# Two heads of batch 0's keys by the hardware queues in place of four, w_in ahead of batch 1's keys, and a new order of the work

## The chip, the cores and the metric

The kernel runs on one core of one Trainium2 chip. Five engines work side by side: PE (matmuls; it also spends time on loading weights), DVE and ACT (elementwise work; both can read PE's results), POOL (GpSimd) and SP. Transfers from and to the chip's memory are issued by SP and ACT (the hardware queues) and by POOL (GpSimd's queue, which can convert float32 to bfloat16 on the way). The metric is the device time of one execution in microseconds; the time before is the median of three runs.

## The reference

Eight batches of eight heads with 576 rows of 64 go through two attentions and a feed-forward layer. In the first attention 32 learned rows p ask the keys and values; its result serves as keys and as values for the second attention, in which the queries ask. The heads are then put side by side, which gives 4608 rows of 512, and pass through w_in, an activation, and w_out.

```
p_packed = sm_attn(p, k, v)            # softmax(scale * p k^T) v, 32 rows per head
out      = sm_attn(q, p_packed, p_packed)
x = out.transpose(0, 2, 1, 3).reshape(B * S, H * D)
h = x @ w_in
g = where(h >= 1, h, where(h <= -1, 0, (h + 1)**2 / 4))
return g @ w_out
```

All inputs and the output are float32; the kernel computes with bfloat16 operands.

## The kernel before

All of q, k, v, w_in and w_out is converted to bfloat16. For each batch b the steps, by the names of the tiles, are:

- `kT`, `qT`: keys and queries with the head dimension on the partitions. For batches 0 and 1 PE transposes them into a PSUM tile `tp` (in the functions `turned`, L377), and DVE and ACT copy the halves out. From batch 2 on SP issues a transposing transfer.
- `sp`, `ex`, `pk`, `ppT`: scores of p against the keys (L431), their exponentials on ACT (L437), and the pack, i.e. the product with the values, and the row sums (L476 to L486), copied out as `ppT`.
- `s`, `eT`, `sm`, `ln`, `rc`, `A`: scores of the queries against the packed rows (L516), exponentials (ACT, L556), their sums by a matmul with ones (L561), a reciprocal by logarithm and exponential (ACT, L565, L570), and the normalized weights `A` (DVE, L575), for the two groups g of heads.
- `mp`, `M`: the packed rows times w_in (L529), in four quarters f of 512 columns, copied out as `M` (helper `copy`, L197). The product of attention and w_in is thus taken as `A` times `M`, and the attention's output itself is never formed.
- `h`, `x`, `t`, `hT`: for each of 16 slices fi of 128 of the 2048 columns, four matmuls of `M` and `A` (L649), two steps of the activation on ACT or ACT and DVE (x, L655; t, L663 on DVE or L665 on ACT), and a last one on DVE (hT, L670). Slices 0 to 3 need quarter 0 of M, 4 to 7 quarter 1, and so on.
- `o`, `ob`: 36 output tiles of 128 rows, each 16 matmuls of hT with w_out (L723), copied out and stored by SP (L741). Slices 0 to 3 need quarter 0 of w_out, and so on.

The PSUM is divided into three wide tiles (`w`), which `tp`, `sp`, `pk`, `s`, `sm`, `mp`, `h` and a few output tiles (those in `LENT`) take in turns, and two narrow ones (`o`). A wide tile is free again when the copy or the activation that reads it has ended.

The order of the work on each engine is not written out. Every step is a `Task` with a rank, the engines that could do it with a cost on each, and the steps that it needs; `Plan.run` plays through them with these costs and fixes one list per engine, which each engine then works off in order. The ranks come from the constants `H1`, `H2`, `T1`, `T2`, `EARLY` and so on. Where PE has nothing to do in the plan before the first output matmul, the function `warm` puts in matmuls of zeros (L791), as many as fill the planned gap.

The loads stand in the order of `LOADS`, one list on POOL's queue. In before it is k0 (its heads 4 to 7), v0, q0 (three pieces), k1, w_in quarters 0 (two halves), v1, and so on. Heads 0 to 3 of batch 0's keys, and p for batches 0 and 1, are loaded ahead of them as float32 by the hardware queues, two heads by SP and two by ACT (`k_raw`, L317), and converted by DVE and ACT (`casts`). There is one buffer for keys (`k`), so that k1's load waits until k0's transposes are done. `MB0` and `MB1` are costs of single loads in the plan; they change what the plan expects, not the transfer.

Of the kernel before, what the change touches and what calls it, by code (L numbers as in the profile page):

```python
# [121 lines left out]
def kernel(  # L122
# [11 lines left out]
    f32 = mybir.dt.float32  # L134
# [4 lines left out]
    B, H, S, D = q.shape  # L139
# [8 lines left out]
    G, Q, TP, X = 2, 4, 96, 2  # L148
    NC = S // TP
# [3 lines left out]
    FW = 512  # L153
    NF = d_ff // FW
    SPAN = 28.0
    MB0 = {("k", 0, 4): 1.07, ("v", 0, 0): 1.35, ("q", 0, 0): 0.5}
    MB1 = {("w_in", 0, 0): 0.7, ("w_in", 0, 1): 0.7}
    FIRST = 2
    PAIRED = 2
    SPLIT, AHALF, WPARTS, MPARTS, QLATE, ORDER3, ORDER, MERGE = 0, 0, 1, 3, 0, 0, 2, 3  # L160
    Q0 = [range(0, 8, 2), range(1, 5, 2), range(5, 9, 2)]
    LOADS = "k0 v0 q0 k1 win0 v1 win1 win2 wout0 wout1 win3 wout2 q1 wout3 v2 q2 p k2"
    H1, H2 = 26.53, 38.72
    PITCH0, PITCH1 = 0.56, 0.33
    T1, T2 = -11.47, 25.95
    LENT = [1, 8]
    L1, M1 = -14.28, 5.97
    KT1, QT1 = -33.50, -6.64
    SC1, PK1 = 25.09, -6.06
    ST1, MT1 = 12.93, 25.80  # L170
    EARLY = [[(27.88, 73.23), (29.26, 41.94), (45.63, 29.37), (44.78, 16.76)], [(54.77, 7.14), (14.06, 35.17), (62.97, 47.75), (30.5, 10.14), (23.52, 36.85)]]

    V, A_, G_ = nc.vector, nc.scalar, nc.gpsimd
    nc.scalar.preload_act_table_set("natural_log_exp_and_others")
# [1 line left out]
    BUFS = dict(w=3, o=2, k=1, q=2, v=1, vv=1, kT=2, qT=2, ex=2, ppT=2, M=2, A=2, eT=4, ln=2, rc=2, x=4, t=4, ob=4)  # L176
    const = ctx.enter_context(tc.tile_pool(name="const", bufs=1))
    work = ctx.enter_context(tc.tile_pool(name="work", bufs=1))
# [7 lines left out]
    def new(tag, shape, dtype):  # L186
        return work.tile(shape, dtype, tag=tag, name=tag, bufs=BUFS[tag])

    plan = Plan(dict(BUFS, dma=8))
# [14 lines left out]
    def either(dve, act, *pairs, parted=None):  # L204

        def emit(e):
            for to, of in pairs:
                copy(e, to(), of(), parted)
        return {"DVE": (dve[0], dve[1], emit), "ACT": (act[0], act[1], emit)}
# [1 line left out]

    p_raw = work.tile([NP, 2, H, D], f32, tag="k1", name="p_raw", bufs=1)
    p_nat = const.tile([NP, B, H, D], bf16)
    k_raw = work.tile([TP, 4, NC * D], f32, tag="q", name="k_raw", bufs=BUFS["q"])
    w_in_sb = const.tile([P, Q, d_ff], bf16)
    w_out_sb = const.tile([P, KF, d_model], bf16)
    w_in_v = moe_w_in.rearrange("(a p) f -> p a f", p=P)
# [22 lines left out]
    landed = {}  # L240
# [9 lines left out]
    def dma(key, rank, emit, mb, takes=(), settle=0.9):  # L250
        t = plan.add(rank, {"DMA": (0.78, 2.1, emit, mb / 0.405, settle)}, takes=list(takes) + ["dma"])
        plan.release("dma", [t])
        chain("loads", t)
        landed[key] = t
        if key == ("v", 0, 0):
            chain("loads", identity)
        return t

    def tokens(nm, b):
        if (nm, b) not in have:  # L260
            have[nm, b] = new(nm, [TP, H, NC, D], bf16)
        return have[nm, b].rearrange("p h c d -> p h (c d)")

    def heads(hs):
        return slice(hs[0], hs[-1] + 1, hs.step)

    def rows_of(nm, b, hs):
        return {"k": k, "q": q, "v": v}[nm][b, heads(hs)].rearrange("h (p c) d -> p h (c d)", c=NC)

    def load(nm, b, rank):  # L270

        for i, hs in enumerate({("k", 0): [range(4, 8)], ("q", 0): Q0}.get((nm, b), [range(H)])):
            def emit(e, hs=hs):
                G_.dma_start(tokens(nm, b)[:, heads(hs)], rows_of(nm, b, hs))  # L274
            mb = MB0.get((nm, b, hs[0]), (1.18 if b < 2 else 1.3) * len(hs) / H)
            t = dma((nm, b, hs[0]), rank + 0.01 * i, emit, mb, [nm] if i == 0 else [], 0.9 if b < 2 else 1.7)
            for h in hs:
                landed[nm, b, h] = [t]
# [16 lines left out]

    for n, what in enumerate(LOADS.split()):
        if what[:-1] == "win":
            load_w_in(int(what[-1]), -1000 + n)
        elif what[:-1] == "wout":
            load_w_out(int(what[-1]), -1000 + n)  # L300
        elif what == "p":
            load_p(-1000 + n)
        else:
            load(what[0], int(what[1]), -1000 + n)
    for b in range(3, B):
        for n, nm in enumerate(["kqv", "kvq", "qkv", "qvk", "vkq", "vqk"][ORDER3 if b == 3 else ORDER]):
            load(nm, b, -960 + 10 * b + n)
# [5 lines left out]
    p_first = plan.add(-1000, {"SP": (1.0, 3.3, load_p_raw)})  # L313

    def load_k_raw(e):
        for i, queue in enumerate((nc.sync, nc.scalar)):
            queue.dma_start(k_raw[:, 2 * i:2 * i + 2], rows_of("k", 0, range(2 * i, 2 * i + 2)))  # L317

    k_first = plan.add(-999, {"SP": (1.0, 4.3, load_k_raw)}, behind=[p_first])
    casts = [plan.add(-30.2 + 0.1 * i, either(  # L320
        (0.5, 0.55), (0.8, 0.85), (lambda i=i: tokens("k", 0)[:, 2 * i:2 * i + 2], lambda i=i: k_raw[:, 2 * i:2 * i + 2])),
        [k_first], behind=landed["k", 0, 4]) for i in range(2)]
    for h in range(4):
        landed["k", 0, h] = casts


    pT_of = {}
# [379 lines left out]
    def output(pr, i, rank, pitch, parts=1):  # L707


        w = d_model // parts  # L710
        lent = pr == 0 and i in LENT
        bs = sorted({2 * pr + i * P // S, 2 * pr + ((i + 1) * P - 1) // S})
# [46 lines left out]
    def evenly(n, start, span):  # L759
        return [(start + span / n * j, span / n) for j in range(n)]  # L760

    for b in range(B):
# [8 lines left out]
        first = 0 if b % 2 == 0 else 4  # L771
        for j, (start, span) in enumerate(EARLY[b] if b < len(EARLY) else evenly(4 + b % 2, base[b] + SPAN, SPAN)):
            parts = 2 if (b, first + j) == (B - 1, 8) else 1
# [53 lines left out]
```

## Time and profile before

| | us |
|---|---|
| median of three runs | 246.61 (246.17 to 246.77) |
| the profiled execution, its own time | 248.54 |
| its span, first to last instruction | 246.8 |
| PE busy | 239.2, 97% |
| ACT busy | 199.0, 81% |
| DVE busy | 177.0, 72% |
| first h matmul | 23.32 |
| first o matmul | 32.51 |
| last matmul's end | 243.0 |
| mean granted clock of PE | 0.993 |

The engines' busy times and the chain of waits are those of one profiled execution. A matmul's end is modelled, so that matmuls of one group overlap in the rows; the distance from one start to the next is what PE spends on it. Rows of windows give busy times in a stretch of the span; rows of the timeline give start, duration, engine, line, operation, output tile and input tiles, count, and in brackets the idle time ahead and what ended it.

### The profile page before, as it was taken

What the parts mean: (1) busy time and instruction counts of PE and PEld (TensorE: products, weight loads), DVE (VectorE), ACT (ScalarE), POOL (GpSimd) and SP (SyncE); (2) the same over time, 40 slices, a digit from 0 to 9 for tenths busy, and PEclk for the clock granted to TensorE, in tenths of its full rate; (3) what the DMA queues carried; (4) which work ended last, traced back from release to release, by engine and by line L of the source; (5) the groups of instructions that cost most, each with busy time, mean ns of one, the idle gap of its engine ahead of it and who ended that gap; (6) DMA issues with size and microseconds to landing.
All of it is one profiled execution on the core that took longest, in us unless ns stands there. A gap on an engine that the chain in (4) does not pass through costs nothing.

```text
span 246.8 us, 5485 instructions
## 1 busy us (share of the span) xinstructions
PE 239.2 (97%) x2221; PEld 137.6 (56%) x2221; DVE 177.0 (72%) x299; ACT 199.0 (81%) x329; POOL 29.0 (12%) x42
## 2 busy tenths in 40 slices
PE   8979999999999999999999999999999999999993
PEld 2745555465654665566556646655665455555453
DVE  4425996588966997799889859957995877776000
ACT  3575997899989989999899799979988998886111
POOL 7463410000500120021021001100000000000000
PEclk9997999999999999999999999999999999999999
DMA  7999999969999999999999959976721111122223
GB/s 162 201 204 206 206 206 205 194 119 155 161 215 240 199 168 224 174 141 218 234 139 215 177 104 147 181 129 120 137 63 46 43 45 43 44 51 77 54 76 85
DMA packets 59195, 35.85 MB, mean 145 GB/s; under 512 B 31905, under 2 KB 54689, under 8 KB 59169
## 3 DMA queue, kind: packets, MB, share of 16 engines
q0 software_dynamic: 24256, 18.25, 49.9%
q1 hardware_dynamic: 34208, 16.69, 32.1%
q10 hardware_dynamic: 704, 0.56, 0.8%
q8 instruction: 17, 0.28, 0.5%
q14 instruction: 10, 0.07, 0.1%
HBM read 37.22 MB, written 9.44 MB: 189 GB/s over the span
## 4 chain that ended last, share of the span: by engine, by line
PE 87%; DMA 6%; ACT 4%; DVE 1%; issue 0%
PE o L723 49%; PE h L649 25%; DMA k<-in_k_dram 4%; PE mp L529 3%; PE sp L431 2%; DMA k_raw<-in_k_dram 2%; PE pk L476 2%; PE tp L377 1%; PE o L791 1%; PE sm L561 1%; PE s L516 1%; DVE M L197 1%; ACT x L655 1%; PE pk L486 1%; ACT eT L556 1%; ACT rc L570 1%
## 5 line engine op out<-in xcount | busy, mean ns | idle before, releaser
L723 PE MATMUL o<-w_out_sb,hT 128*128 128x512 bf16 (+1 forms) x592 | 146.9, 373 | 0.0
L670 DVE SCALAR_TENSOR_TENSOR hT<-t 128x576 bf16<-128x576 f32 x128 | 93.8, 753 | 9.1 <-ACT t L665 7.0
L655 ACT ACTIVATE x<-h 128x576 f32<-128x576 f32 x128 | 79.1, 659 | 10.9 <-PE h L649 9.5
L723 PEld LDWEIGHTS <-hT 128*128 128x128 bf16 x592 | 55.6, 98 | 48.2 <-issue 4.9
L649 PE MATMUL h<-A,M 128*128 128x288 bf16 x512 | 79.0, 286 | 0.4 <-DVE M L197 0.4
L649 PEld LDWEIGHTS <-M 128*128 128x128 bf16 x512 | 49.5, 98 | 29.2 <-issue 1.4
L665 ACT ACTIVATE t<-x 128x576 f32<-128x576 f32 x63 | 43.8, 695 | 1.1
L663 DVE TENSOR_SCALAR t<-x 128x576 f32<-128x576 f32 x65 | 30.8, 473 | 9.7 <-ACT x L655 9.5
L197 ACT CAST M<-mp 128x1024 bf16<-128x1024 f32 (+1 forms) x24 | 22.7, 977 | 3.5 <-PE mp L529 3.4
L197 DVE COPY ob<-o 128x512 f32<-128x512 f32 x24 | 16.4, 688 | 7.8 <-PE o L723 7.6
L575 DVE SCALAR_TENSOR_TENSOR A<-eT,rs,rc 128x576 bf16<-128x576 bf16 x16 | 12.9, 816 | 9.0 <-ACT rc L570 9.0
L197 ACT COPY ob<-o 128x512 f32<-128x512 f32 (+1 forms) x13 | 7.2, 557 | 14.6 <-PE o L723 14.3
L274 POOL DMA_DIRECT2D k<-in_k_dram x8 | 6.5, 811 | 104.7 <-DMA kT<-k 81.1
L791 PE MATMUL o<-zeros 128*128 128x512 bf16 (+1 forms) x45 | 13.8, 421 | 1.2 <-DVE zeros L227 1.2
L437 ACT ACTIVATE ex<-sp 96x768 bf16<-96x768 f32 x16 | 12.5, 804 | 2.6 <-PE sp L431 2.6
L197 DVE CAST M<-mp 128x1024 bf16<-128x1024 f32 (+1 forms) x11 | 11.2, 1025 | 1.3 <-PE mp L529 1.3
L556 ACT ACTIVATE eT<-s,rs 128x576 bf16<-128x576 f32 x16 | 11.0, 744 | 0.7 <-PE s L516 0.7
L529 PE MATMUL mp<-w_in_sb,ppT 64*32 64x512 bf16 x256 | 11.3, 387 | 0.0
L570 ACT ACTIVATE rc<-ln 128x576 f32<-128x576 f32 x16 | 10.7, 686 | 0.3
L565 ACT ACTIVATE ln<-sm 128x576 f32<-128x576 f32 x16 | 10.2, 649 | 0.1
L431 PEld LDWEIGHTS <-kT 128*128 128x128 bf16 x192 | 8.1, 104 | 2.8 <-DVE kT L197 0.5
L197 ACT CAST ppT<-pk 64x128 bf16<-64x128 f32 x22 | 5.7, 260 | 4.0 <-PE pk L486 3.6
(50 smaller groups left out, 114.3 us busy)
## 6 DMA issues: line engine op xcount, KB each, us to landing
v<-in_v_dram POOLq DMA_DIRECT2D x8, 576.0 KB, 10.6
out_dram<-ob SPq DMA_DIRECT2D x23, 192.0 KB, 3.4
k<-in_k_dram POOLq DMA_DIRECT2D x7, 576.0 KB, 8.7
q<-in_q_dram POOLq DMA_DIRECT2D x7, 576.0 KB, 12.9
out_dram<-ob SPq DMA_DIRECT2D x24, 128.0 KB, 2.4
w_out_sb<-in_moe_w_out_dram POOLq DMA_DIRECT2D x4, 512.0 KB, 18.2
w_in_sb<-in_moe_w_in_dram POOLq DMA_DIRECT2D x3, 512.0 KB, 13.8
out_dram<-ob SPq DMA_DIRECT2D x23, 64.0 KB, 2.6
```

Of the source, the lines that this page charges most:

```text
L197: i = (nc.vector.tensor_copy if e == "DVE" else nc.scalar.copy)(to, of)
L431: nc.tensor.matmul(o, kT[:, j * TP:j * TP + w], pT[:, b, g, 2 * i + a], start=True, stop=True)
L529: nc.tensor.matmul(have["mp", b, f][a * NP:(a + 1) * NP, g], have["ppT", b][r, g, a], w_in_sb[r, a, f * FW:(f + 1) * FW], start=True, stop ...
L556: nc.scalar.activation(have["eT", b, g], have["s2", b, g][:, :, :HALF], AF.Exp, scale=rs_of[b][:, g, 1:])
L570: nc.scalar.activation(have["rc", b, g][:, xs], have["ln", b, g][:, xs], AF.Exp, scale=-1.0)
L649: nc.tensor.matmul(have["h", b, fi][:, hf, :HALF], have["M", b][:, g, fi * P:(fi + 1) * P], have["A", b][:, g, hf], start=(g == 0), stop=( ...
L655: nc.scalar.activation(have["x", b, fi][:, hs[0]:hs[-1] + 1], have["h", b, fi][:, hs[0]:hs[-1] + 1, :HALF], AF.Prelu, bias=-1.0, alpha=0.5)
L663: V.tensor_scalar(t, x, 1.0, 0.0, ALU.add, ALU.max)
L665: nc.scalar.activation(t, x, AF.Relu, bias=1.0)
L670: V.scalar_tensor_tensor(dst, t, 1.0, t, ALU.min, ALU.mult)
L723: nc.tensor.matmul(have["o", key][:, :w], hT[:, fi, i * P:(i + 1) * P], w_out_sb[:, fi, cols], start=(fi == 0), stop=(fi == KF - 1))
L791: nc.tensor.matmul(o[:, :w], zeros[:, :P], zeros[:, :w], start=True, stop=True)
```

## The change

`KR` is new: the number of heads of batch 0's keys that come as float32 by the hardware queues. It is 2, one head for SP and one for ACT, in place of 4. Heads 2 and 3 come by a load of their own on POOL's queue, ahead of the one for heads 4 to 7. The scores of heads 0 to 3 therefore need the two casts and this load.

In `LOADS`, three quarters of w_in stand ahead of k1, and v1 stands behind k1 and the first quarter of w_out; further back q2, v2, k2 and p change places. All other constants of the order are other numbers, so that every list is a new one. `SPLIT = 2` cuts h, x, t and hT of batch 0's slices 0 and 1 in two halves. `MPARTS = 2` leaves only quarters 0 and 1 of batch 0's M to be copied in two pieces (three quarters before). `MERGE = 2` puts the first quarter of mp beside the scores s from batch 2 on (from batch 3 on before). `LENT` gives wide tiles to the output tiles 2 and 5 in place of 1 and 8. `ORDER3` sets the order of batch 3's loads.

```diff
-    MB0 = {("k", 0, 4): 1.07, ("v", 0, 0): 1.35, ("q", 0, 0): 0.5}
+    KR = 2
+    MB0 = {("k", 0, 2): 0.33, ("k", 0, 4): 0.59, ("v", 0, 0): 1.24, ("q", 0, 0): 0.5}
...
-    SPLIT, AHALF, WPARTS, MPARTS, QLATE, ORDER3, ORDER, MERGE = 0, 0, 1, 3, 0, 0, 2, 3
+    SPLIT, AHALF, WPARTS, MPARTS, QLATE, ORDER3, ORDER, MERGE = 2, 0, 1, 2, 0, 4, 2, 2
...
-    LOADS = "k0 v0 q0 k1 win0 v1 win1 win2 wout0 wout1 win3 wout2 q1 wout3 v2 q2 p k2"
-    H1, H2 = 26.53, 38.72
...
-    LENT = [1, 8]
...
+    LOADS = "k0 v0 q0 win0 win1 win2 k1 wout0 v1 wout1 win3 wout2 q1 wout3 q2 v2 k2 p"
+    H1, H2 = 22.12, 44.98
...
+    LENT = [2, 5]
...
-    k_raw = work.tile([TP, 4, NC * D], f32, tag="q", name="k_raw", bufs=BUFS["q"])
+    k_raw = work.tile([TP, KR, NC * D], f32, tag="q", name="k_raw", bufs=BUFS["q"])
...
-        for i, hs in enumerate({("k", 0): [range(4, 8)], ("q", 0): Q0}.get((nm, b), [range(H)])):
+        for i, hs in enumerate({("k", 0): [range(KR, 4), range(4, 8)], ("q", 0): Q0}.get((nm, b), [range(H)])):
...
-            queue.dma_start(k_raw[:, 2 * i:2 * i + 2], rows_of("k", 0, range(2 * i, 2 * i + 2)))
+            queue.dma_start(k_raw[:, i:i + 1], rows_of("k", 0, range(i, i + 1)))
...
-        (0.5, 0.55), (0.8, 0.85), (lambda i=i: tokens("k", 0)[:, 2 * i:2 * i + 2], lambda i=i: k_raw[:, 2 * i:2 * i + 2])),
-        [k_first], behind=landed["k", 0, 4]) for i in range(2)]
+        (0.3, 0.35), (0.45, 0.5), (lambda i=i: tokens("k", 0)[:, i:i + 1], lambda i=i: k_raw[:, i:i + 1])),
+        [k_first], behind=landed["k", 0, 4]) for i in range(KR)]
     for h in range(4):
-        landed["k", 0, h] = casts
+        landed["k", 0, h] = casts + landed["k", 0, KR]
```

On POOL, from the first load on, the list was as follows (96x4x384 is four heads of keys, 96x8x384 a whole batch's k, v or q, 128x4x512 a quarter of w_in or w_out):

```order
L274 DMA k<-in_k_dram 96x4x384
L274 DMA v<-in_v_dram 96x8x384
masks.py:197 MEMSET ident 128x128
masks.py:199 ISA
masks.py:199 AFFINE_SELECT ident<-ident 128x128
L274 DMA q<-in_q_dram 96x4x384
L274 DMA q<-in_q_dram 96x2x384 x2
L274 DMA k<-in_k_dram 96x8x384
L285 DMA w_in_sb<-in_moe_w_in_dram 64x4x512 x2
L274 DMA v<-in_v_dram 96x8x384
L285 DMA w_in_sb<-in_moe_w_in_dram 128x4x512 x2
```

The same place of POOL's list now:

```order
L275 DMA k<-in_k_dram 96x2x384
L275 DMA k<-in_k_dram 96x4x384
L275 DMA v<-in_v_dram 96x8x384
masks.py:197 MEMSET ident 128x128
masks.py:199 ISA
masks.py:199 AFFINE_SELECT ident<-ident 128x128
L275 DMA q<-in_q_dram 96x4x384
L275 DMA q<-in_q_dram 96x2x384 x2
L286 DMA w_in_sb<-in_moe_w_in_dram 64x4x512 x2
L286 DMA w_in_sb<-in_moe_w_in_dram 128x4x512 x2
L275 DMA k<-in_k_dram 96x8x384
L291 DMA w_out_sb<-in_moe_w_out_dram 128x4x512
```

A load of two heads is new at the front, and batch 1's keys have moved behind three quarters of w_in; v1, not shown, follows the quarter of w_out.

On ACT, from batch 0's logarithms on, the list was as follows (kT and ex are those of batch 1, x and t those of batch 0's slices):

```order
L565 ACTIVATE ln<-sm 128x576 x2
L570 ACTIVATE rc<-ln 128x576
L197 COPY kT<-tp 128x4x96 x2
L570 ACTIVATE rc<-ln 128x576
L437 ACTIVATE ex<-sp 96x12x64 x2
L655 ACTIVATE x<-h 128x576 x3
L665 ACTIVATE t<-x 128x576
L197 CAST ppT<-pk 64x128 x4
```

The same place of ACT's list now:

```order
L566 ACTIVATE ln<-sm 128x576 x2
L571 ACTIVATE rc<-ln 128x576 x2
L198 CAST M<-mp 128x512
L656 ACTIVATE x<-h 128x288 x4
L666 ACTIVATE t<-x 128x288
L656 ACTIVATE x<-h 128x576 x2
L666 ACTIVATE t<-x 128x576 x2
L656 ACTIVATE x<-h 128x576 x3
L198 COPY kT<-tp 128x4x96 x2
L666 ACTIVATE t<-x 128x576
L438 ACTIVATE ex<-sp 96x12x64 x2
```

The two rc follow each other, and batch 1's keys and their exponentials have moved behind the x of seven slices of batch 0. PE's list has the same move: batch 1's transposes, which stood ahead of batch 0's mp and h, stand behind h of slice 6.

On DVE, from batch 0's last copies of queries on, the list was:

```order
L197 COPY qT<-tp 128x288 x2
L197 COPY kT<-tp 128x4x192 x2
L575 SCALAR_TENSOR_TENSOR A<-eT,rs,rc 128x576
L197 CAST M<-mp 128x512
L575 SCALAR_TENSOR_TENSOR A<-eT,rs,rc 128x576
```

The same place of DVE's list now:

```order
L198 COPY qT<-tp 128x288 x2
L198 CAST M<-mp 128x512 x2
L576 SCALAR_TENSOR_TENSOR A<-eT,rs,rc 128x576 x2
L198 CAST M<-mp 128x512
L664 TENSOR_SCALAR t<-x 128x288 x2
```

Both copies of M's quarter 0 have moved ahead of the first A, and batch 1's kT copies out of this place.

More of the change, by code (lines that the diff above doesn't have):

```diff
@@ L159 @@
     PAIRED = 2
-    SPLIT, AHALF, WPARTS, MPARTS, QLATE, ORDER3, ORDER, MERGE = 0, 0, 1, 3, 0, 0, 2, 3
+    SPLIT, AHALF, WPARTS, MPARTS, QLATE, ORDER3, ORDER, MERGE = 2, 0, 1, 2, 0, 4, 2, 2
     Q0 = [range(0, 8, 2), range(1, 5, 2), range(5, 9, 2)]
-    LOADS = "k0 v0 q0 k1 win0 v1 win1 win2 wout0 wout1 win3 wout2 q1 wout3 v2 q2 p k2"
-    H1, H2 = 26.53, 38.72
-    PITCH0, PITCH1 = 0.56, 0.33
-    T1, T2 = -11.47, 25.95
-    LENT = [1, 8]
[L167 to L171, printed above, removed]
+    LOADS = "k0 v0 q0 win0 win1 win2 k1 wout0 v1 wout1 win3 wout2 q1 wout3 q2 v2 k2 p"
+    H1, H2 = 22.12, 44.98
+    PITCH0, PITCH1 = 2.02, 0.20
+    T1, T2 = -12.12, 26.79
+    LENT = [2, 5]
+    L1, M1 = -0.94, -0.23
+    KT1, QT1 = -5.40, 11.05
+    SC1, PK1 = 23.87, 1.56
+    ST1, MT1 = 34.14, 40.50
+    EARLY = [[(11.06, 92.69), (49.64, 36.28), (46.46, 38.0), (38.16, 25.3)], [(56.52, 5.8), (23.31, 23.03), (58.69, 13.54), (38.34, 20.24), (1.0, 50.02)]]
     V, A_, G_ = nc.vector, nc.scalar, nc.gpsimd
@@ L316, in load_k_raw @@
         for i, queue in enumerate((nc.sync, nc.scalar)):
-            queue.dma_start(k_raw[:, 2 * i:2 * i + 2], rows_of("k", 0, range(2 * i, 2 * i + 2)))
-    k_first = plan.add(-999, {"SP": (1.0, 4.3, load_k_raw)}, behind=[p_first])
+            queue.dma_start(k_raw[:, i:i + 1], rows_of("k", 0, range(i, i + 1)))
+    k_first = plan.add(-999, {"SP": (1.0, 3.3, load_k_raw)}, behind=[p_first])
     casts = [plan.add(-30.2 + 0.1 * i, either(
-        (0.5, 0.55), (0.8, 0.85), (lambda i=i: tokens("k", 0)[:, 2 * i:2 * i + 2], lambda i=i: k_raw[:, 2 * i:2 * i + 2])),
-        [k_first], behind=landed["k", 0, 4]) for i in range(2)]
+        (0.3, 0.35), (0.45, 0.5), (lambda i=i: tokens("k", 0)[:, i:i + 1], lambda i=i: k_raw[:, i:i + 1])),
+        [k_first], behind=landed["k", 0, 4]) for i in range(KR)]
     for h in range(4):
-        landed["k", 0, h] = casts
+        landed["k", 0, h] = casts + landed["k", 0, KR]
     pT_of = {}
```

## The prediction

> **What bounds the kernel now.** I read the page's busy shares first, then windows over the whole span, then the timelines of PE, ACT, DVE and POOL and the DMA issues of the first 45 us.
>
> ```profile
> PE 239.2 (97%) x2221; PEld 137.6 (56%) x2221; DVE 177.0 (72%) x299; ACT 199.0 (81%) x329; POOL 29.0 (12%) x42
> ```
>
> ```profile
> 5.00:30.00 25.00, 22.43 (x350) 13.70 (x349) 13.81 (x27) 17.48 (x35) 11.28 (x17) 0.93 1.28 204
> 31.00:243.00 212.00, 211.94 (x1852) 122.16 (x1844) 160.05 (x262) 178.84 (x292) 13.00 (x16) 1.00 0.80 140
> 15.65:17.40 1.75, 0.00 (x1) 0.00 (x0) 0.00 (x0) 1.04 (x2) 0.00 (x0) 1.00 1.25 204
> 19.00:22.50 3.50, 3.50 (x36) 1.71 (x34) 2.41 (x4) 2.33 (x4) 1.20 (x3) 0.51 1.28 206
> ```
>
> The columns of a window are its length, then the busy time of PE, PEld, DVE, ACT and POOL, the granted clock, the DMA share and GB/s. From 31 to 243 us PE is busy 211.94 of 212.00, so a change wins or loses before that, and a lead that PE has by then stays until the end. Two losses stand in the head: PE is idle from 15.65 to 17.4 us, and behind that the clock is 0.51 until 22.5 us.
>
> ```profile
> 4.67 1.62 PE L791 MATMUL o<-zeros 128*128 128x512 bf16 x5
> ...
> 12.84 0.43 PE L377 MATMUL tp<-ident,q 96*128 96x96 bf16 x6
> ...
> 17.48 1.19 PE L377 MATMUL tp<-ident,k 96*128 96x96 bf16 x24 [1.83 <-DMA k<-in_k_dram]
> ...
> 23.32 1.63 PE L649 MATMUL h<-A,M 128*128 128x288 bf16 x12
> ...
> 39.59 1.14 PE L649 MATMUL h<-A,M 128*128 128x288 bf16 x8
> ...
> 50.91 0.65 PE L649 MATMUL h<-A,M 128*128 128x288 bf16 x4
> 51.40 0.38 PE L723 MATMUL o<-w_out_sb,hT 128*128 128x512 bf16 x1
> 51.62 0.65 PE L649 MATMUL h<-A,M 128*128 128x288 bf16 x4
> ```
>
> PE waits 1.83 us for batch 1's keys, which stand in its list ahead of batch 0's feed-forward. Start to start, four h matmuls take 0.49 us and one o matmul 0.22. ACT has the keys in its list too:
>
> ```profile
> 16.02 0.67 ACT L570 ACTIVATE rc<-ln 128x576 f32<-128x576 f32 x1
> 18.20 0.99 ACT L197 COPY kT<-tp 128x384 bf16<-128x384 bf16 x2 [1.51 <-PE tp L377]
> 19.09 0.69 ACT L570 ACTIVATE rc<-ln 128x576 f32<-128x576 f32 x1
> ...
> 20.89 0.81 DVE L575 SCALAR_TENSOR_TENSOR A<-eT,rs,rc 128x576 bf16<-128x576 bf16 x1
> 22.67 0.69 DVE L197 CAST M<-mp 128x512 bf16<-128x512 f32 x1 [0.98 <-PE mp L529]
> ```
>
> The second rc stands behind the copies of the late keys, so the second A ends at 21.7 and the first h starts at 23.32.
>
> **The DMA stream.** GpSimd's queue moves everything after the first 5 us.
>
> ```profile
> 1.30 0.81 POOL L274 DMA_DIRECT2D k<-in_k_dram  x1 [0.86 <-POOLq L811]
> ...
> 3.43 2.36 POOL L274 DMA_DIRECT2D q<-in_q_dram  x3
> ```
>
> ```profile
> q10 hardware_dynamic: 480, 0.36, 23.6%
> q1 hardware_dynamic: 480, 0.36, 22.9%
> ...
> q0 software_dynamic: 26, 0.02, 63.9%
> ```
>
> ```profile
> k<-in_k_dram POOLq DMA_DIRECT2D x1, 288.0 KB, 5.6
> v<-in_v_dram POOLq DMA_DIRECT2D x1, 576.0 KB, 7.8
> q<-in_q_dram POOLq DMA_DIRECT2D x2, 144.0 KB, 7.6
> k<-in_k_dram POOLq DMA_DIRECT2D x1, 576.0 KB, 9.0
> w_in_sb<-in_moe_w_in_dram POOLq DMA_DIRECT2D x2, 256.0 KB, 9.1
> q<-in_q_dram POOLq DMA_DIRECT2D x1, 576.0 KB, 20.9
> ```
>
> The second fence is the hardware queues up to 6 us (packets, MB) and GpSimd's queue, q0, between 4.6 and 4.8 us, its first real traffic, 3.3 us after its first issue. The third fence gives microseconds from issue to landing for the issues at 1.3, 2.1, 4.5 to 5.2, 8.39, 9.2 to 9.8 and 19.41 us (the last is batch 1's q). At 204 GB/s, 200 KB in a microsecond, a line from 4.6 us gives the end of each transfer's data: k0's half 6.0, v0 8.9, q0 11.8, k1 14.7, w_in 0 17.2, q1 38.4. They land at 6.9, 9.9, 12.6, 17.4, 18.9 and 40.3: 0.8 to 1.0 later at first, 1.7 to 1.9 later once the queue is deep (k1 alone 2.7).
>
> **The change, part by part.**
>
> *Loads.* The queue gets 144 KB more (two heads in bfloat16) and one more issue; the hardware queues carry 288 KB less of float32. Where the queue's traffic now starts the trace doesn't show. If it counts from the first issue, it is 4.6 as before. If it waited for the hardware queues, which moved 0.72 MB from 1.9 to 5.0 us and now have 0.29 MB less, it is 1.2 us earlier, 3.4. The first issue is a smaller one (two heads; such a one of q takes about 0.65 us, against 0.81), so I take 4.4, near the first bound, since nothing in the rows ties the two kinds of queue together. The line then gives landings (+0.9 up to q0, +1.7 for w_in 0, +1.9 behind): k0's heads 2 and 3 at 6.0, its other half 7.5, v0 10.4, q0 13.2, w_in 0 16.6, w_in 1 19.3, w_in 2 21.9, k1 24.8, w_out 0 27.3, v1 30.2, w_out 1 32.8, w_in 3 35.3, w_out 2 37.9, q1 40.8. POOL's new issue shifts v0, the identity and q0 by 0.65 to 0.8 us. The transfers are limited by the stream and not by issues, and p's transposes, which need the identity, have zero matmuls in front of them: nothing, at most 0.1 us without that cover. The waits of later issues fall on transfers eight issues back and are over while some 1,500 KB are still queued.
>
> The Trainium skill (DMA: Bandwidth & Descriptors, Specifications) gives about 1 us to the first byte on GpSimd's path; the 3.3 us of this trace disagree. By the page's figure, as an estimate, the landings would be 2 us earlier and the sum up to 2 us lower.
>
> *Batch 0's head.* The last of heads 0 to 3 was ready when this cast ended, at 6.66:
>
> ```profile
> 5.83 0.83 ACT L197 CAST k<-k_raw 96x768 bf16<-96x768 f32 x1 [0.31 <-DMA k_raw<-in_k_dram]
> ```
>
> Now they are there at 6.0, the landing of heads 2 and 3 (0 and 1 come in less float32 and are cast by then). But their scores stand ahead of the other half's transposes, and ACT copies that half only behind the first exp, so the first pack gains nothing and may come some 0.2 us later. It doesn't matter, because q0's last part lands 13.2 against 12.6, and PE takes it at once (12.84 before): +0.4. From there the list is as before up to the first rc (16.02 + 0.4); the second follows directly and ends at 17.65, not 19.8. On DVE both copies of M's first quarter now stand ahead of A: w_in 0's second half at 16.6 gives mp until 17.0, its copy (0.69) until 17.65, A to 18.45 and 19.25. PE burns that time with ten zero matmuls. Next in its list is mp of quarter 1, which needs w_in 1 at 19.3. So h starts at 19.7, against 23.32.
>
> *The list behind it*, which now holds k1's transposes and scores. ACT sets the pace, since three wide PSUM tiles are all there are and each is freed by an x:
>
> ```profile
> L655 ACT ACTIVATE x<-h 128x576 f32<-128x576 f32 x128 | 79.1, 659 | 10.9 <-PE h L649 9.5
> L665 ACT ACTIVATE t<-x 128x576 f32<-128x576 f32 x63 | 43.8, 695 | 1.1
> ```
>
> ACT from 19.85: copy of M 0.55, four half x, one half t (halves: 0.33 to 0.66, I take 0.37, near half the work), x2 and x3 0.62 each, t2, t3, x4 (ends 25.4), x5 26.0, x6 26.65, the two kT copies to 27.6. PE with that: h0 to h3 19.7 to 21.7; mp of quarter 2 at 21.95 (w_in 2 at 21.9); h4 to h6 22.95, 23.55, 24.05; k1's transposes at 25.45 and 26.05 (tiles of x4 and x5; keys landed 24.8); h7 26.7; scores 27.25; first o 27.65 (w_out 0 27.3); scores 27.85; four o, h8, o, h9, o until 30.5; batch 1's pack 30.5 to 31.7 (v1 30.2); h10, h11 to 32.7; four o to 33.5 (w_out 1 32.8); sixteen mp to 34.35; seven o; mp of quarter 3 at 35.9 (w_in 3 35.3); six o; h12 at 37.6. Before, h12 stands at 39.59 with the same work done but one o of 0.22 fewer. **Lead: 39.59 + 0.22 - 37.6 = 2.2 us.** The next gate, q1's transposes, comes at 41.1, q1 lands at 40.8.
>
> *The rest.* Halving h0 and h1, another order of later loads, other slots for output tiles and batch 2's first mp beside its scores change no amount of PE work; I cost them at nothing under PE's full cover (211.94 of 212.00 above). Without that cover, a stretch of five h in a row in batch 2 would wait 0.66 - 0.49 = 0.17 us for each h behind the third: 0.3 to 0.5 us.
>
> **The sum.** 246.8 - 2.2 = 244.6 for the span, 248.54 - 2.2 = 246.3 for the profiled execution. That one is 1.9 us above the median of the runs, 246.61; on the median, 244.4.
>
> **The rivals.**
>
> *The stream becomes the bound and the kernel slower.* From 30 to 41 us PE takes each block only 0.1 to 0.7 us after my landing: v1, w_out 1, w_in 3, w_out 2, q1. v1 comes 8 us later than before and stands ahead of h10. Every microsecond that the stream is late beyond those margins is one of idle PE. The lead is gone at 2.3 to 2.8 us late, and 0.7 us are lost at 3.3, that is if the stream gave 178 KB/us instead of 200 up to 33 us. Against it: 204 and 206 GB/s in the rows above. For it: k1's landing alone was 0.8 late. Time: 246.6 + 0.8 = 247.4.
>
> *The clock drops early.* Before, 1.75 us idle and 1.0 us of transposes within 3.4 us were followed by 3.4 us at half clock. Now two zero matmuls in place of five follow p's transposes, and PE stands still from 5.1 (4.67 and twice 0.22) to 6.0 for heads 2 and 3, then transposes 12, waits, transposes 12: some 2 us of such time between 5.1 and 8.5. At half clock the zero matmuls, transposes and scores there take about 1.5 us more; q0's late landing hides 0.4 of it, 1.1 us reach the chain. Time: 245.5. Against it: less of such time than in the stretch that was followed by the drop.
> The Trainium skill's TensorE: Matmul & The Clock Gate says under HAM oscillation that gaps over some 3.4 us throttle again, by which nothing drops now, and in Part 4 that transposes don't count as busy in the same way. A drop after a gap of 1.83 us contradicts the first taken alone and fits the second, which would let it drop here.
>
> *The lead is given back.* q1's margin is 0.3, and ACT's chain of x, t and copies holds no slack from 20 to 30 us; an op that waits in its in-order list could cost 2 us in sum. The page's ACT share, 81% with idle times of 10.9 before x, speaks against it. Time 246.5, no change.
>
> **How the numbers follow.** 0.60 for the forecast, 0.14 for the clock, 0.11 for given back, 0.15 for the slower stream. Faster by over 0.3% (0.74 us, about what a measurement of this kernel can tell from no change) takes the first two: 0.74; 0.11 same; 0.15 slower. The forecast's own range: a start at 3.4 us moves the head and every landing by 1.0, which makes 243.4 (landings 0.9 behind the data gain little more, since rc then holds A); k1's 2.7 for all, half x of 0.62 and the five h: 245.5. For 8 in 10 the range goes on over the clock case and given back: 243.4 to 246.8.
>
> **What would show it.** Right: no PE idle beside k1's transposes before 20 us, clock 1.00 between 19 and 22.5, first h near 19.7, k1's transposes at 25 to 26, h12 near 37.6, v1 landing about 30. Wrong: PE idle before pk of batch 1, mp of quarter 3 or q1's transposes, each released by a DMA (stream); clock 0.50 between 5 and 12 us; or h4 to h7 over 1 us apart (ACT). The prediction falls if the queue's first packets come after 5 us, or if PE shows idle time behind 45 us.

## The result and the profile after

The changed kernel takes 247.77 us in the median (247.06 to 248.97, 20 runs), the kernel before 246.6 beside it (246.17 to 249.0, 20 runs): a ratio of 1.0042 with a 95% interval of 1.0028 to 1.0056. It is slower by 1.0 us by the ratio, 1.2 by the medians; the forecast was 244.4, faster by 2.2. Its profiled execution took 247.79 us, with a span of 246.0, so that unlike the one of before it stands for the median. Of the kernel before about 1 execution in 20 took 1 to 2.4 us more than the median, and of the changed one 3 in 20 took about 1 us more; where the clock of these is on record it is 0.992 or 0.993, and the execution on which the prediction rests, with 0.993, was one of them.

The page's busy times and two of the windows that were shown of before (columns: length, busy time of PE, PEld, DVE, ACT and POOL, granted clock, DMA share, GB/s):

```profile
PE 235.8 (96%) x2185; PEld 137.2 (56%) x2222; DVE 177.5 (72%) x301; ACT 196.6 (80%) x332; POOL 29.3 (12%) x43
```

```profile
15.65:17.40 1.75, 1.75 (x21) 0.89 (x20) 0.00 (x0) 1.75 (x4) 1.25 (x2) 1.00 1.21 199
19.00:22.50 3.50, 3.45 (x26) 1.75 (x26) 2.79 (x4) 1.13 (x4) 0.79 (x1) 1.00 1.27 204
```

The trace lacks 37 matmul records, so PE's 235.8 is too low and says nothing. The windows say what was forecast: PE no longer stands still from 15.65 to 17.4 us, and the clock is 1.00 where it was 0.51. PE's timeline shows waits at other places:

```profile
8.77 0.68 PE L378 MATMUL tp<-ident,k 96*128 96x96 bf16 x12 [1.02 <-DMA k<-in_k_dram]
...
11.70 0.93 PE L482 MATMUL pk<-ex,v 96*64 96x32 bf16 x48 [0.19 <-DMA v<-in_v_dram]
...
14.10 0.43 PE L378 MATMUL tp<-ident,q 96*128 96x96 bf16 x6 [0.27 <-DMA q<-in_q_dram]
...
15.15 0.32 PE L517 MATMUL s<-qT,ppT 64*32 64x288 bf16 x8
...
21.45 2.13 PE L650 MATMUL h<-A,M 128*128 128x288 bf16 x16
...
26.65 1.19 PE L378 MATMUL tp<-ident,k 96*128 96x96 bf16 x24
...
37.70 0.41 PE L530 MATMUL mp<-w_in_sb,ppT 64*32 64x512 bf16 x8 [0.59 <-DVE M L198]
...
39.35 1.14 PE L650 MATMUL h<-A,M 128*128 128x288 bf16 x8
```

Before 15 us PE waits for three loads of batch 0, together 1.48 us. The first h starts at 21.45, not at 19.7, and h12 at 39.35, not at 37.6. GpSimd's queue, which carries those loads, in the changed kernel (microseconds from issue to landing):

```profile
v<-in_v_dram POOLq DMA_DIRECT2D x1, 576.0 KB, 8.9
k<-in_k_dram POOLq DMA_DIRECT2D x1, 288.0 KB, 6.7
q<-in_q_dram POOLq DMA_DIRECT2D x2, 144.0 KB, 9.0
...
k<-in_k_dram POOLq DMA_DIRECT2D x1, 144.0 KB, 3.8
```

Issued at 1.3, 2.0 and 2.74 us, heads 2 and 3 land at 5.1, heads 4 to 7 at 8.7 and v0 at 11.6; the prediction had 6.0, 7.5 and 10.4. And the queue's traffic from 4.5 to 7 us (packets, MB, share):

```profile
q0 software_dynamic: 380, 0.28, 100.2%
```

At 200 KB in a microsecond, the rate that the prediction went by, it would be 0.50 MB.

### The profile page after: what moved, and what is told of

Same layout as the page of the kernel before. It is cut to its first block, busy times and chain, and to the rows that moved or that the text cites. A ratio compares the mean times of both kernels' runs of the same rounds, so it can differ in the third digit from the quotient of the medians.

```text
span 246.0 us, 5479 instructions
## 1 busy us (share of the span) xinstructions
PE 235.8 (96%) x2185; PEld 137.2 (56%) x2222; DVE 177.5 (72%) x301; ACT 196.6 (80%) x332; POOL 29.3 (12%) x43
## 4 chain that ended last, share of the span: by engine, by line
PE 80%; DVE 7%; ACT 4%; DMA 4%; issue 2%; POOL 1%; ACTq 0%; POOLq 0%
PE o L724 46%; PE h L650 21%; DMA q<-in_q_dram 4%; DVE hT L671 3%; PE mp L530 3%; ACT x L656 3%; PE sp L432 2%; PE sm L562 2%; DVE t L664 2%; PE o L792 1%; PE pk L477 1%; PE s L517 1%; DVE M L198 1%; PE tp L378 1%; PE pk L487 1%
## 5 line engine op out<-in xcount | busy, mean ns | idle before, releaser
L724 PE MATMUL o<-w_out_sb,hT 128*128 128x512 bf16 (+1 forms) x559 | 142.3, 373 | 2.1 <-issue 0.8
L671 DVE SCALAR_TENSOR_TENSOR hT<-t 128x576 bf16<-128x576 f32 (+1 forms) x130 | 94.0, 744 | 9.2 <-ACT t L666 7.0
L656 ACT ACTIVATE x<-h 128x576 f32<-128x576 f32 (+1 forms) x130 | 78.9, 654 | 7.4 <-PE h L650 5.7
L666 ACT ACTIVATE t<-x 128x576 f32<-128x576 f32 (+1 forms) x62 | 42.9, 694 | 1.0
L664 DVE TENSOR_SCALAR t<-x 128x576 f32<-128x576 f32 (+1 forms) x68 | 31.6, 465 | 10.4 <-ACT x L656 10.2
L198 ACT CAST M<-mp 128x1024 bf16<-128x1024 f32 (+1 forms) x20 | 19.1, 991 | 5.1 <-PE mp L530 5.0
L198 ACT COPY ob<-o 128x512 f32<-128x512 f32 (+1 forms) x19 | 11.0, 577 | 14.7 <-PE o L724 14.5
L198 DVE CAST M<-mp 128x1024 bf16<-128x1024 f32 (+1 forms) x14 | 15.5, 1107 | 4.1 <-PE mp L530 4.1
L198 DVE COPY ob<-o 128x512 f32<-128x512 f32 x18 | 12.4, 690 | 6.1 <-PE o L724 5.5
L438 ACT ACTIVATE ex<-sp 96x768 bf16<-96x768 f32 x16 | 12.3, 802 | 3.1 <-PE sp L432 3.1
L275 POOL DMA_DIRECT2D v<-in_v_dram x8 | 6.5, 817 | 43.1 <-DVE vv L464 36.5
## 6 DMA issues: line engine op xcount, KB each, us to landing
w_in_sb<-in_moe_w_in_dram POOLq DMA_DIRECT2D x3, 512.0 KB, 13.2
```

The costliest lines, as they stand in the source:

```text
L198: i = (nc.vector.tensor_copy if e == "DVE" else nc.scalar.copy)(to, of)
L438: nc.scalar.activation(have["ex", b][:, :, 64 * i:64 * i + 64], have["sp", b, i][:TP, :E * X * G], AF.Exp, scale=scale)
L656: nc.scalar.activation(have["x", b, fi][:, hs[0]:hs[-1] + 1], have["h", b, fi][:, hs[0]:hs[-1] + 1, :HALF], AF.Prelu, bias=-1.0, alpha=0.5)
L664: V.tensor_scalar(t, x, 1.0, 0.0, ALU.add, ALU.max)
L666: nc.scalar.activation(t, x, AF.Relu, bias=1.0)
L671: V.scalar_tensor_tensor(dst, t, 1.0, t, ALU.min, ALU.mult)
```

## The experiments

### What the kernel before usually does

`e1_before_again` is the kernel before, unchanged.

> The kernel before, unchanged. Theory A (the profile of before was an execution with the clock drop, and the usual one has none): time near 246.6 with a mean clock of 0.998 or more in most runs, about 1 to 2 us more in the runs whose clock is 0.992 to 0.994; PE still waits some 1.8 us for batch 1's keys near 16 us, and the h of slice 12 starts near 37.7, not 39.6. Theory B (the drop comes in every execution and its cost is hidden): clock 0.993 also at 246.6 us, h of slice 12 near 39.6.

246.59 us (246.06 to 247.2, 10 runs; ratio 0.9986, 0.9976 to 0.9996). Its profiled execution took 246.48 us with a clock of 1.0. PE's timeline:

```profile
16.93 1.19 PE L377 MATMUL tp<-ident,k 96*128 96x96 bf16 x24 [0.96 <-DMA k<-in_k_dram]
...
21.29 1.63 PE L649 MATMUL h<-A,M 128*128 128x288 bf16 x12
...
37.56 1.14 PE L649 MATMUL h<-A,M 128*128 128x288 bf16 x8
```

Batch 1's keys are awaited for 0.96 us, not 1.83 as in the first profile and as expected here, no clock drop follows, and h12 starts at 37.56, not at 39.59. The 2.03 us between the two belong to a rare execution, and nearly all that the change was to win lay in them. What makes it rare was not tested; the traces show that PE's work ahead of the keys ends 0.32 us later in e1 and that the keys come 0.55 us earlier, which together is the shorter wait.

### The two parts of the change, each alone

`e2_new_order_old_loads` has the changed kernel's order of the work, with batch 0's keys loaded as before.

```diff
-    k_raw = work.tile([TP, KR, NC * D], f32, tag="q", name="k_raw", bufs=BUFS["q"])
+    k_raw = work.tile([TP, 4, NC * D], f32, tag="q", name="k_raw", bufs=BUFS["q"])
...
+                if (nm, b, hs[0]) == ("k", 0, KR):
+                    return
...
-            queue.dma_start(k_raw[:, i:i + 1], rows_of("k", 0, range(i, i + 1)))
+            queue.dma_start(k_raw[:, 2 * i:2 * i + 2], rows_of("k", 0, range(2 * i, 2 * i + 2)))
```

> The changed kernel's order of the work on every engine, with the loads of batch 0's keys as before (four heads as float32 on the hardware queues, no load of two heads by GpSimd). Theory L (the loss comes from the load of two heads, which leaves a hole in GpSimd's stream): the stream runs on from 4.5 us, q0's last part lands near 12.7 instead of 14.1 to 14.6, first h near 20 instead of 21.45, time 246.0 (245.8 to 246.4), below before. Theory O (the new order itself costs the microsecond): time 247.5 to 247.9 whatever the loads do.

246.61 us (246.03 to 247.72, 10 runs; ratio 1.0005, 0.9988 to 1.0022). PE's timeline:

```profile
13.62 0.32 PE L519 MATMUL s<-qT,ppT 64*32 64x288 bf16 x8
...
19.91 2.13 PE L652 MATMUL h<-A,M 128*128 128x288 bf16 x16
...
36.25 0.41 PE L532 MATMUL mp<-w_in_sb,ppT 64*32 64x512 bf16 x8 [0.58 <-DVE M L198]
...
37.89 1.14 PE L652 MATMUL h<-A,M 128*128 128x288 bf16 x8
```

With the order the same and only the loads different, the changed kernel is 1.53 us later at the first s (15.15), 1.54 at the first h, 1.46 at h12 and 1.5 in its span (244.5 here). In the medians it is 1.16. What comes 1.55 us later is the last part of q0, for which PE waits in both kernels before the first s (shown further down). That the changed kernel's three waits add up to nearly the same 1.48 us is a coincidence: e2 itself is idle for 1.20 us before 7 us, when it waits for the casts of heads 0 to 3. The time is that of the kernel before and not the 246.0 expected of it, so the new order alone neither wins nor loses: against the usual execution of before it reaches the first h 1.38 us earlier (19.91 against 21.29), and at h12 nothing is left (37.89, with one o of 0.22 more done, against 37.56).

`e3_old_order_new_loads` is the other half: the order of before, and the loads as changed.

```diff
+                if (nm, b) == ("k", 0):
+                    G_.dma_start(tokens(nm, b)[:, 2:4], rows_of(nm, b, range(2, 4)))
...
-            queue.dma_start(k_raw[:, 2 * i:2 * i + 2], rows_of("k", 0, range(2 * i, 2 * i + 2)))
+            queue.dma_start(k_raw[:, i:i + 1], rows_of("k", 0, range(i, i + 1)))
```

> The order of the work of before, with the changed loads alone (two heads as float32 on the hardware queues, two by a load of their own on GpSimd's queue ahead of the other four). Theory L: the same hole between 4.5 and 8 us, batch 1's keys land 1.2 to 1.8 us later, time 247.8 to 248.4. Theory O: 246.6 as before.

247.84 us (247.15 to 248.02, 5 runs; ratio 1.0025, 0.9989 to 1.0062). The interval is wide and includes no change, so the time alone shows no loss. Its fastest execution, which is the profiled one, has the same mark as the changed kernel:

```profile
7.77 0.68 PE L379 MATMUL tp<-ident,k 96*128 96x96 bf16 x12 [0.80 <-DMA k<-in_k_dram]
...
21.94 1.63 PE L651 MATMUL h<-A,M 128*128 128x288 bf16 x12
```

The first h is 0.65 us later than the old loads give it with this order (21.29).

### What makes GpSimd's queue late

`e4_one_load_of_six` is the changed kernel with heads 2 to 7 in one load on GpSimd's queue in place of two.

```diff
+                if (nm, b) == ("k", 0):
+                    if hs[0] != KR:
+                        return
+                    hs = range(KR, H)
```

> The changed kernel with heads 2 to 7 of batch 0's keys in one load on GpSimd's queue instead of two loads (heads 2 and 3, heads 4 to 7). Same bytes. Theory L in its form that a short first transfer drains before the next one follows: the stream starts near 4.5 us and runs on at 200 KB/us; q0's last part lands near 13.3; heads 2 and 3 come with the rest at 7.5, which delays the first scores but not the queries; first h near 20.2, time 246.2 to 246.8. If the hole comes from the bytes that moved from the hardware queues to GpSimd's, whatever the number of loads: hole as in the changed kernel, time 247.8 or more. Theory O: 247.8.

248.95 us (248.76 to 249.87, 4 runs; ratio 1.0097, 1.0074 to 1.012). The queue runs at full rate here, from 4.5 to 7 us:

```profile
q0 software_dynamic: 574, 0.43, 120.9%
```

But heads 2 and 3 now come only with the rest, so PE waits for them, and behind the wait the clock is 0.50 (windows as above):

```profile
7.90 0.60 PE L382 MATMUL tp<-ident,k 96*128 96x96 bf16 x10 [2.09 <-DMA k<-in_k_dram]
```

```profile
8.00:10.00 2.00, 2.00 (x31) 1.39 (x31) 0.56 (x1) 0.66 (x2) 0.75 (x1) 0.86 1.30 199
10.00:12.00 2.00, 2.00 (x14) 1.14 (x12) 0.95 (x2) 1.11 (x2) 0.69 (x1) 0.50 1.31 201
```

`e5_more_on_hw_queues` is the changed kernel with two heads on each hardware queue again, of which one is loaded and not read; the small load on GpSimd's queue stays.

```diff
-            queue.dma_start(k_raw[:, i:i + 1], rows_of("k", 0, range(i, i + 1)))
+            queue.dma_start(k_raw[:, 2 * i:2 * i + 2], rows_of("k", 0, range(i, i + 3, 2)))
```

> The changed kernel with 288 KB per hardware queue as before (each brings one head that is used and one that nobody reads), GpSimd's loads as changed. Theory S (the hole comes from the short first load, which drains before the next one is posted): the hole between 4.5 and 8 us stays, q0's last part lands 14.0 to 14.6, time 247.6 to 248.2. Theory R (the hole comes from the relief of the hardware queues, which lets GpSimd's stream start at 3.4 us, before enough of it is posted): the stream starts near 4.5 us with 144, 288 and 576 KB posted, runs on at 120 to 130 packets in half a microsecond, q0's last part lands near 13.3, time 246.7 to 247.2.

247.93 us (247.38 to 249.12, 8 runs; ratio 1.0056, 1.0031 to 1.008). The queue starts at 4.5 us, as before, and is nearly at full rate at once (4.5 to 7 us):

```profile
q0 software_dynamic: 543, 0.40, 106.3%
```

The time is not lower. Its heads 0 and 1 come late again (PE begins the first transposes at 6.67, against 5.62 in the changed kernel), and the 144 KB of heads 2 and 3 still stand ahead of v0 and q0. How much each of these costs is not shown: the profiled execution took 249.12 us, 1.2 above the median, and PE was at half rate in it until 13 us (last section). So this run separates the two causes in the stream, but not in the time.

`e6_old_k_in_two_loads` is the kernel before with its load of heads 4 to 7 cut in two.

```diff
+                if (nm, b) == ("k", 0):
+                    G_.dma_start(tokens(nm, b)[:, 4:6], rows_of(nm, b, range(4, 6)))
+                    hs = range(6, 8)
```

> The kernel before with its load of heads 4 to 7 cut in two loads of two heads on GpSimd's queue; the bytes of every queue and the order are those of before. Theory S: the stream starts near 3.4 to 4 us and has the hole, batch 1's keys land about 1 us later, time 247.3 to 248. Theory R: stream from 4.5 us without a hole, one issue of 0.65 us more that the stream hides, time 246.6 to 247.0.

246.95 us (246.21 to 249.0, 10 runs; ratio 1.0022, 1.0 to 1.0045). The queue starts at 4.5 us, as before. One more short load at the front by itself costs 0.3 us by the medians and 0.5 by the ratio, and the interval reaches down to no change.

`e9_identity_first` is the changed kernel with POOL's making of the identity moved ahead of its first load.

```diff
-    identity = plan.add(-998.5, {"POOL": (0.6, 1.25, lambda e: make_identity(nc, ident))})
+    identity = plan.add(-998.5, {"POOL": (0.6, 1.25, lambda e: None)})
...
+                if (nm, b, hs[0]) == ("k", 0, KR):
+                    make_identity(nc, ident)
```

> The changed kernel with one edit: POOL makes the identity (0.9 us with its overhead) ahead of its first load and not behind the load of v0, so that every load of batch 0 on GpSimd's queue is issued 0.8 to 0.9 us later. In the changed kernel GpSimd's packets begin at 3.4 us and then run at half rate from 4.5 to 7 us. Theory S (the hole comes from starting while the hardware queues are still at work): the first packets come at 4.3 or later, no half microsecond after 5 has fewer than 105 packets, heads 4 to 7 land at 7.8 to 8.3 in place of 8.7, PE waits 0.6 us or less for them, time 246.9 to 247.4. Theory F (the hole follows the queue's own start, about one microsecond behind its first packet): it moves with the start, heads 4 to 7 land at 9.5 to 9.7, PE waits 1.8 to 2.0 us, its clock may be halved behind it, time 248.5 or more. Theory T (something at that time of the program slows the queue, whatever its start): fewer than 100 packets from 5.5 to 7 us, heads 4 to 7 at 8.9 to 9.2, time 247.9 to 248.2.

247.46 us (246.93 to 248.83, 11 runs; ratio 1.0048, 1.003 to 1.0066). The run didn't test what it was made for. POOL stands idle until 1.3 us in the changed kernel, so the identity fits in there and the first load moves by only 0.2 us, to 1.49:

```profile
0.74 0.20 POOL masks.py:197 MEMSET ident<- 128x128 bf16 x1 [0.29 <-POOLq L814]
1.02 0.29 POOL masks.py:199 TENSOR_SCALAR_AFFINE_SELECT ident<-ident 128x128 bf16<-128x128 bf16 x1
1.49 1.45 POOL L277 DMA_DIRECT2D k<-in_k_dram  x2 [0.19 <-issue]
2.93 0.79 POOL L277 DMA_DIRECT2D v<-in_v_dram  x1
3.70 2.29 POOL L277 DMA_DIRECT2D q<-in_q_dram  x3
```

The queue still starts at 3.4 us and moves only 0.32 MB from 4.5 to 7. The three theories stay undecided by it. With q0's loads issued 0.7 us earlier (3.70 against 4.39) the first h comes at 21.13.

The stream in one profiled execution of each kernel, from the same view (GpSimd's queue from 4.5 to 7 us):

| kernel | its first packets, us | keys of batch 0 on it | MB from 4.5 to 7 us |
|---|---|---|---|
| before; e1; e2 | 4.5 | one load of 4 heads | 0.44; 0.42; 0.41 |
| e4 | 3.5 | one load of 6 | 0.43 |
| e6 | 4.5 | two of 2 | 0.38 |
| e5 | 4.5 | 2, then 4 | 0.40 |
| e3, e9, e10 | 3.4 | 2, then 4 | 0.37; 0.32; 0.32 |
| after | 3.4 | 2, then 4 | 0.28 |

An early start alone (e4) doesn't slow the queue, and two loads alone (e5, e6) slow it by some 0.03 MB. Only both together take 0.05 to 0.14 MB, 0.25 to 0.7 us at 200 KB/us. Why they do is open: what one packet waits for there the traces don't say.

### The order behind it

`e7_new_numbers_old_loads_planned` is the kernel before with all of the changed kernel's constants of the order, but its own loads of batch 0's keys, so that the plan knows of them.

```diff
-    LOADS = "k0 v0 q0 k1 win0 v1 win1 win2 wout0 wout1 win3 wout2 q1 wout3 v2 q2 p k2"
-    H1, H2 = 26.53, 38.72
...
-    LENT = [1, 8]
...
+    LOADS = "k0 v0 q0 win0 win1 win2 k1 wout0 v1 wout1 win3 wout2 q1 wout3 q2 v2 k2 p"
+    H1, H2 = 22.12, 44.98
...
+    LENT = [2, 5]
```

> The kernel before with all numbers of the new order (LOADS, H1 to EARLY, SPLIT, MPARTS, MERGE, LENT), the loads of batch 0's keys and their costs left as before, so that the order is planned for them. The loads alone separate it from the changed kernel. Theory L+P (the loads cost the changed kernel 1.2 to 1.5 us; the new order's earlier h is lost again until slice 12, 0.6 us of it where quarter 3 of mp waits for a wide PSUM tile): first h near 19.9, mp of quarter 3 idle near 0.6 us before 36.3, time 246.3 to 246.8. If the order itself were a gain of the predicted 2 us: 244.6 to 245.

246.20 us (245.84 to 246.68, 10 runs; ratio 0.9985, 0.9972 to 0.9998): faster than the changed kernel, and than the kernel before by an interval that ends just short of no change. PE's timeline:

```profile
19.97 2.13 PE L649 MATMUL h<-A,M 128*128 128x288 bf16 x16
...
36.09 0.41 PE L529 MATMUL mp<-w_in_sb,ppT 64*32 64x512 bf16 x8 [0.59 <-DVE M L197]
...
37.73 1.14 PE L649 MATMUL h<-A,M 128*128 128x288 bf16 x8
```

The 0.59 us stand in every kernel with this order. `mp` of batch 0's quarter 3 needs a wide PSUM tile; the output tile 2, which has a wide tile by `LENT`, holds one, and the others are free only when DVE has copied batch 1's M.

`e8_quarter3_ahead` puts batch 1's second quarter of mp (quarter 1) behind batch 0's quarter 3, for which it is taken out of its pair with quarter 0.

```diff
+        groups = [[f] for f in range(NF)] if fine else [[0], [1], [2, 3]] if b == 1 else [[1, 2, 3]] if merged else [[0, 1], [2, 3]]
...
+                             mode="s", behind=[before] + ([f3_of[0]] if (b, fs) == (1, [1]) else []))
...
+                if (b, fs) == (0, [3]):
+                    f3_of[0] = t
```

> The kernel of the run before this, with batch 1's quarter 1 of mp put behind batch 0's quarter 3, so that quarter 3 finds a free wide PSUM tile. Theory P (the wait of 0.58 us at quarter 3 is for a PSUM tile that batch 1's copy frees, and PE has nothing else in front): the wait goes, h of slice 12 0.4 to 0.6 us earlier, time 0.3 to 0.6 us below the run before. Rival (the wait is w_in 3's landing): the wait stays, time unchanged.

246.57 us (246.37 to 247.26, 10 runs; ratio 1.0003, 0.9985 to 1.0021). PE's timeline:

```profile
37.15 1.15 PE L652 MATMUL h<-A,M 128*128 128x288 bf16 x8
...
70.55 0.44 PE L517 MATMUL s<-qT,ppT 64*32 64x288 bf16 x16
...
90.64 0.44 PE L517 MATMUL s<-qT,ppT 64*32 64x288 bf16 x16
...
183.86 0.44 PE L517 MATMUL s<-qT,ppT 64*32 64x288 bf16 x16
```

The wait is gone and h12 is 0.58 us earlier than in e7, but the time is not lower. The scores s of batches 2, 3 and 7, in e7:

```profile
70.91 0.44 PE L516 MATMUL s<-qT,ppT 64*32 64x288 bf16 x16
...
94.84 0.44 PE L516 MATMUL s<-qT,ppT 64*32 64x288 bf16 x16
...
183.53 0.44 PE L516 MATMUL s<-qT,ppT 64*32 64x288 bf16 x16
```

At 70 us e8 still leads by 0.36; at 184 it is 0.33 behind, and no view shows PE idle between. The edit changed the plan around 33 us, and the plan then put batch 3's scores 4 us earlier among the h and o matmuls: from there on it is another list. What in it costs 0.7 us is not told apart.

### Both again

`e10_changed_again` is the changed kernel once more, without an edit.

> The changed kernel as it is, beside the others of this call: 247.6 to 247.9 in the median, 1.0 to 1.3 us above the kernel before; its profile has the hole of GpSimd's queue between 4.5 and 7 us again and three waits of PE on loads that add up to 1.3 to 1.6 us.

247.76 us (247.49 to 248.25, 6 runs; ratio 1.0056, 1.0035 to 1.0078). The time and the slow stream (0.32 MB) are as expected; the three waits are not there, since PE was at half rate in their place (shown below). q0's last part, for which PE waits until 14.61 us, sets the first h at 21.26 all the same.

`e11_planned_again` is the kernel of e7 once more, without an edit.

> The kernel before with the changed kernel's numbers of the order and its own loads of batch 0's keys, run again beside the changed kernel: if its first ten times were no luck, 246.1 to 246.4, 0.2 to 0.5 us below the kernel before and 1.3 to 1.6 below the changed kernel; if they were, the same as the kernel before.

246.26 us (246.02 to 246.7, 12 runs; ratio 0.999, 0.9978 to 1.0002), 0.3 us under the kernel before and 1.5 under the changed one beside it. The version with the new order and the old loads has the lowest median of all. Its gain over the kernel before is 0.25 to 0.4 us by the two ratios, half of the 0.74 taken above as the bound of what can be told from no change, and the second interval includes none.

## Why the prediction was wrong

**The base of the sum: 2.0 us.** The lead of 2.2 us was measured from the h12 of the one profiled execution (39.59) and subtracted from the median of the runs (246.61), although that execution stood 1.9 us above the median. The text put both numbers side by side and didn't ask whether the 1.9 were the very loss that the change removes. They were: in a usual execution h12 stands at 37.56 (e1). From there the same walk gives 37.56 + 0.22 - 37.6 = 0.2 us, that is 246.4.

**The loads, as in the rival of the slower stream, but earlier: 1.2 to 1.5 us.** The step *Loads* took a start at 4.4 us and 200 KB/us from there, which put q0's end at 13.2 us. The start was better than that, at 3.4, and the rate was worse, 0.28 MB in 2.5 us, so that by 8 us the queue had moved 0.60 MB, no more than in e2 with its start at 4.5 (0.61; e10 has 0.64):

```profile
q0 software_dynamic: 811, 0.60, 95.8%
```

```profile
q0 software_dynamic: 815, 0.61, 85.1%
```

The first row is the changed kernel from 3 to 8 us, the second e2. From 8 to 12 us both queues run alike, the changed kernel's first:

```profile
q0 software_dynamic: 1078, 0.80, 130.9%
```

```profile
q0 software_dynamic: 1092, 0.80, 131.0%
```

By 12 us each has moved 1.40 to 1.41 MB. The end of q0 is at 1.62 MB of the changed kernel's stream and at 1.47 MB of e2's. At 0.2 MB in a microsecond, and if the loads move in their order, the data are complete at 13.1 and 12.3 us: the 144 KB more count in full, 0.8 us as an estimate. But PE gets q0's last part 1.55 us later than in e2. The loading of its weights (PEld) in the changed kernel and in e2:

```profile
14.79 0.28 PEld L378 LDWEIGHTS <-q 96*128 96x128 bf16 x6 [0.33 <-DMA q<-in_q_dram]
```

```profile
13.24 0.30 PEld L380 LDWEIGHTS <-q 96*128 96x128 bf16 x6 [0.22 <-DMA q<-in_q_dram]
```

So the bytes are about half of it. The other half is the time from the last data to the landing: the prediction added 0.9 us for it up to q0, which holds in e2, and in the changed kernel it is about 1.7. Why it is longer there is open. The rival had the mechanism and its sign, at the wrong place: it looked for the lateness from 30 to 41 us, where every load kept its margin. The first bound for the start, "waited for the hardware queues", was the true one, and no gain.

**Both together account for the result.** 244.4 + 2.0 + 1.2 to 1.5 = 247.6 to 247.9, measured 247.77. That is an addition of two measured differences, and it leaves the new order's own gain at no more than 0.4 us (e7).

**Batch 0's head, right but for its input.** With q0 in time (13.24 in e2, forecast 13.2) the first h starts at 19.91, forecast 19.7. The second rc ends at 17.68, forecast 17.65, and no longer waits for keys. What the walk missed is that PE's second mp waits 0.26 us for DVE's first copy of M.

**The list behind it, nearly right.** From the first h to h12 the forecast had 17.9 us, e2 has 17.98, the changed kernel 17.90. But the walk missed the wait of 0.59 for a wide tile by leaving out the tile lent to output 2; other steps were as much too long, so that the sum came out by luck.

**"A lead that PE has by then stays until the end": true only for the same list.** Between the changed kernel and e2, one list, 1.46 us at h12 are 1.46 at the last s and 1.5 in the span. Between e7 and e8, two lists, a lead of 0.58 becomes a lag. *The rest*, at nothing, rested on PE being busy in 211.94 of 212.00 us, and such a row doesn't show what two lists differ by.

**The early clock drop.** As a rival it was to make the time 245.5. It appears in full where PE waits 2.09 us at one place (e4), and not with 1.02 in the changed kernel. The estimate of idle time and transposes behind it was too crude; that a wait among the transposes can be followed by a drop, e4 shows.

**The identity, costed at nothing.** It is 0.6 us later behind the new load, 1.1 in e10, and p's transposes wait for it, by 0.23 us in e10. With the identity first (e9) the time is 247.46 against 247.76 beside it, within the scatter of both.

## What to carry to other kernels

Ask of a profiled execution that stands well above the median which loss in it makes the difference, before a change gets credit for removing that loss: here the kernel already ran without it in about 19 of 20 executions. Data moved from one queue to another in the first microseconds is not free because it is issued earlier: count what the receiving queue has moved by a fixed time, and follow the last of the loads on which the first dependent chain waits. And a lead in the head is worth its size only if the list of work behind it stays the same; a planner that sees other costs makes another list.

## What was unexpected of the hardware

A granted clock of 1.00 in a window is no proof of full rate in a kernel's first 13 us. In e10, PE's timeline and a window of it:

```profile
1.20 3.17 PE L792 MATMUL o<-zeros 128*128 128x512 bf16 x7 [1.20 <-DVE zeros L228]
4.60 0.37 PE L337 MATMUL tpp<-ident,p_nat 32*128 32x32 bf16 x8 [0.23 <-POOL ident masks.py:199]
...
5.72 1.17 PE L378 MATMUL tp<-ident,k 96*128 96x96 bf16 x12
6.69 1.48 PE L792 MATMUL o<-zeros 128*128 128x512 bf16 x3
7.96 0.87 PE L432 MATMUL sp<-pT,kT 128*128 128x64 bf16 x12
...
10.87 0.53 PE L432 MATMUL sp<-pT,kT 128*128 128x64 bf16 x12
```

```profile
4.90:10.30 5.40, 5.40 (x46) 3.67 (x44) 1.52 (x5) 2.76 (x6) 4.29 (x7) 1.00 1.17 159
```

The zero matmuls stand 0.42 us apart until 8 us (three from 6.69 to 7.96), and the scores take 0.87 where the same group takes 0.53 at 10.87. In the profiled execution of before this rate is left between 5 and 6 us (five zero matmuls in 1.62 us), in e1 later (five in 2.31), in that of e5 not before 13. PE's timeline in e1, and then in e5:

```profile
4.61 2.31 PE L791 MATMUL o<-zeros 128*128 128x512 bf16 x5
```

```profile
12.20 0.87 PE L432 MATMUL sp<-pT,kT 128*128 128x64 bf16 x12
```

The clock records of the traces, which no view lists, settle what the 1.00 means: the first record, full clock each time, is at 5.4 us in before, 6.9 in e1, 10.5 in e10 and 13.1 in e5, which is where the distances shorten, and a window counts the time ahead of the first record as 1.00.

The Trainium skill (TensorE: Matmul & The Clock Gate, Part 1) says that half rate is the state at the start, left after some 3.4 us of steady work counted in a free-running window, so that the same kernel has more or fewer slow matmuls from run to run. The ends at 5.4 and 6.9 us of one and the same kernel agree, with matmuls from 1.2 us on; the ends at 10.5 and 13.1 are later than that figure gives, and why is open. The page also warns that recorded clock events are not to be trusted alone; in these four traces they agree with the distances.

GpSimd's first packets come 2.1 us after the first issue when the hardware queues carry 0.29 MB less, and 3.2 us after it when they don't (3.4 and 4.5 us against an issue at 1.3); one larger load leaves the rate behind that start intact, and a small one ahead of another doesn't.
